# Attention and mixture-of-experts kernel: raw rows of v in the first chunk's coarse product, the local product with v stored with the neighbours innermost, and another order on ScalarE in the lead-in

## The chip, the cores and the metric

The kernel runs on one core of one Trainium2 chip. The metric is the device time of one execution in microseconds; less is better.

## The reference, cut to what matters

```python
# attention: q, k, v are (4, 8, 576, 64)
q_d = q.reshape(B, H, 144, 4, D).mean(axis=3)        # k_d, v_d likewise
out_d = softmax(scale * q_d @ k_d.T) @ v_d           # coarse attention
out_up = np.repeat(out_d, 4, axis=2)
mask = np.abs(pos[:, None] - pos[None, :]) < 4       # each row sees 7 neighbours
out_local = softmax(where(mask, scale * q @ k.T, -1e9)) @ v
x = (out_up + out_local) -> (2304, 512)
# experts: w_gate (512, 8), w1 (8, 512, 1024), w2 (8, 1024, 512)
P = exp(x @ w_gate - max); 8 rounds of row and column normalisation
out = sum over e of P[:, e:e+1] * (relu(x @ w1[e]) @ w2[e])
```

## The kernel before, in words

The 576 positions are taken in groups of four (144 groups for each batch and head). The rows of x are cut into six chunks of groups; the first two have 64 groups (256 rows of x), the next three 128. For a chunk the kernel makes the local attention (seven neighbours for each row, on VectorE, partly on GpSimd), the coarse attention (on TensorE with its softmax on VectorE and ScalarE), and the sum of both, x. The matrix products of the experts run on TensorE meanwhile, on the chunks whose x is ready.

**Experts.** A unit is one expert and 128 of its 1024 hidden columns. `mm1` multiplies x with a piece of w1 (12 matmuls into `psh`: x and w1 are each kept as a high part, `xh` and `w1h`, and a rest, `xl` and `w1l`), `mm2` with a piece of w2 (`psy`). The units of the first four experts run on the first chunk alone (32 units, 256 columns wide); the units after them on the first two chunks together (512 wide). The weights arrive as raw tiles `r`; ScalarE makes the high part (L193), GpSimd the rest (L200), or VectorE, where the planner finds that GpSimd would be late (L203). `hh` (ScalarE) and `hl` (VectorE) are the two parts of the hidden layer after the relu.

**The lead-in** is what comes before the first `psh` matmul: the whole attention of the first chunk. Its tiles in the order of the work: `psq` and `pssum` (sums over four rows of q and k, made by matmuls with the identity), copied by ScalarE to `qf` and `kz`; `pss`, the coarse scores; `nm`, their negated maxima (VectorE); `pp`, exponentials and then the normalised weights (ScalarE, with `sm` from VectorE between); `pst`, their transposes; `pt`, the copy of these (ScalarE); `psv`, the sums over four rows of v (L524), copied to `dv` (L529); `pso`, weights times `dv` (L595); `od`, its copy. Each comes twice, for the two halves hf of the heads. Beside this the local attention: products `prod` of q with neighbours of k (L274), their sums `sc` (L297), a softmax over seven neighbours, products of these weights with neighbours of v (L336), and their sums over the neighbours `lo` (L367). In the first chunk GpSimd makes three of the four products with v. `psx` (L771) transposes `lo`; `xs` adds `od` to it (L779); `xh` and `xl` are its two parts.

**What sets the order.** The program is written by a planner that runs on the host before: each piece of work is a Python generator (a thread) that yields the planned time at which it can go on, or `None` while it has to wait for another thread; at each turn the thread with the lowest time goes on. The planned times come from a clock for each engine (`dve`, `act`, `pool`, `pe`, with fixed costs). So each engine gets one list of instructions, which it executes in order. In the lead-in the threads are `w` (gate weights), `l` (local attention), `q`, `s0`, `s1` (sums of k), `v0`, `v1` (sums of v), `a`, `b` (coarse attention of the two halves) and `x`. After the lead-in the same threads go on between the units, at places that depend on the planned clocks; `pump` in `mm1` and `mm2` lets them in.

The lines that matter most:

```python
in_=pr[:, r0:r0 + nr].rearrange("p r w d -> p r d w"), axis=AX.X, op=ALU.add,   # L367 sum over w
d_sum[0, hf, 2] = (t_sb, done)                                                    # first_v, sums of v ready
vs, t_v = d_sum.pop((0, hf, 2))                                                   # first_d waits for them
while not x_ok(0):                                                                # the lead-in's loop
v_done = (0, 1, 2) in d_sum or 1 in v_set                                         # weights wait for the sums of v
```

## Time and profile before

| | |
|---|---|
| median of 3 runs | 1734.84 us (1732.46 to 1734.93) |
| the profiled execution's own time | 1733.57 us |
| its span in the profile | 1731.8 us |
| TensorE busy | 1691.7 us, 98% of the span |
| VectorE, GpSimd, ScalarE busy | 787.0, 676.9 and 494.8 us |
| first `psh` matmul, first `psy` matmul | at 48.96 us, at 58.26 us |

The profile gives each instruction's engine, line, tiles, start and length, and names what ended an idle time. Times are counted from the start of the span; the execution's own time is 1.8 us more than the span. [...]

### The profile page before, as it was taken

Reading aid. Unit: us, or ns where it says so; the run is one execution under the profiler, and the core shown is the slowest. Engines: PE = TensorE matmul, PEld = TensorE weight load, DVE = VectorE, ACT = ScalarE, POOL = GpSimd, SP = SyncE. Lnnn points to the kernel's source line nnn. Section 1 sums busy time; section 2 is a strip of 40 time slices with the busy share of each in tenths; the row PEclk is TensorE's granted clock in tenths of the full one; section 3 lists DMA queues with packets and bytes.
Section 4 is the critical chain, followed back from the end, with each engine's and each line's share of the span. In section 5 each row is a group of like instructions: output and inputs, shape, how many; then the busy total and the mean of one; then the engine's idle time right before and its main releaser. Section 6 shows DMA issues by size and latency. Waiting matters only on the chain.

```text
span 1731.8 us, 21860 instructions
## 1 busy us (share of the span) xinstructions
PE 1691.7 (98%) x8457; PEld 1405.0 (81%) x8457; DVE 787.0 (45%) x922; ACT 494.8 (29%) x1030; POOL 676.9 (39%) x479
## 2 busy tenths in 40 slices
PE   6988999999999999999999999999999999999998
PEld 4877888788788877888888888888888888888887
DVE  7678887798788784513433421121111111211112
ACT  1554443444344333331121131131131221311210
POOL 5889886587676554440040040040040220401300
PEclk7899999999999999999999999999999999999999
DMA  8786666677577533341251240030030120300101
GB/s 200 197 235 190 170 186 178 169 192 183 154 168 183 138 116 116 115 137 47 73 183 49 67 134 1 0 98 1 0 110 1 37 62 1 97 1 13 49 25 37
DMA packets 177609, 178.12 MB, mean 103 GB/s; under 512 B 10850, under 2 KB 127088, under 8 KB 177506
## 3 DMA queue, kind: packets, MB, share of 16 engines
q1 hardware_dynamic: 166754, 157.33, 34.2%
q10 hardware_dynamic: 10752, 19.40, 3.2%
q8 instruction: 66, 1.08, 0.3%
q14 instruction: 37, 0.30, 0.1%
HBM read 157.29 MB, written 19.40 MB: 102 GB/s over the span
## 4 chain that ended last, share of the span: by engine, by line
PE 78%; issue 10%; POOL 5%; DMA 5%; DVE 2%; ACT 0%; SPq 0%; POOLq 0%; ACTq 0%; DVEq 0%
PE psh L957 38%; PE psy L976 13%; PE psy L978 12%; PE psy L977 12%; DMA r<-in_moe_w_dram 3%; POOL w1l L200 2%; POOL w2l L200 2%; DVE lo L367 1%; POOL dr L449 1%; DMA dr<-in_k_dram 1%; DMA dr<-in_v_dram 1%; PE pss L673 0%; PE psg L808 0%; DMA lq<-in_q_dram 0%; PE psx L771 0%
## 5 line engine op out<-in xcount | busy, mean ns | idle before, releaser
L200 POOL TENSOR_TENSOR w1l<-r,w1h 128x512 fp32r<-128x512 f32 x192 | 280.3, 1460 | 867.6 <-ACT w1h L193 842.7
L966 DVE SCALAR_TENSOR_TENSOR hl<-psh,hh 128x512 fp32r<-128x512 f32 (+1 forms) x352 | 208.5, 592 | 851.7 <-ACT hh L963 851.6
L957 PE MATMUL psh<-xh,w1h 128*128 128x512 f32 (+1 forms) x1408 | 502.7, 357 | 2.7 <-ACT w1h L193 2.1
L957 PE MATMUL psh<-xl,w1h 128*128 128x512 f32 (+1 forms) x1408 | 497.6, 353 | 3.8 <-POOL xl L792 2.0
L957 PE MATMUL psh<-xh,w1l 128*128 128x512 f32 (+1 forms) x1408 | 497.4, 353 | 1.2 <-POOL w1l L200 1.2
L963 ACT ACTIVATE hh<-psh 128x512 fp32r<-128x512 f32 (+1 forms) x352 | 182.7, 519 | 981.2 <-PE psh L957 962.7
L976 PE MATMUL psy<-w2h,hh 128*128 128x512 f32 x1152 | 456.6, 396 | 0.1
L978 PE MATMUL psy<-w2h,hl 128*128 128x512 f32 x1152 | 451.8, 392 | 0.0
L977 PE MATMUL psy<-w2l,hh 128*128 128x512 f32 x1152 | 451.8, 392 | 0.0
L957 PEld LDWEIGHTS psh<-xh,w1h 128*128 128x128 f32 x1408 | 266.9, 190 | 47.0 <-ACT w1h L193 2.5
L957 PEld LDWEIGHTS psh<-xl,w1h 128*128 128x128 f32 x1408 | 267.2, 190 | 45.9 <-DVE xl L795 2.7
L957 PEld LDWEIGHTS psh<-xh,w1l 128*128 128x128 f32 x1408 | 267.1, 190 | 39.2 <-POOL w1l L200 1.8
L200 POOL TENSOR_TENSOR w2l<-r,w2h 128x512 fp32r<-128x512 f32 x183 | 272.5, 1489 | 42.5 <-ACT w2h L193 41.1
L978 PEld LDWEIGHTS psy<-w2h,hl 128*128 128x128 f32 x1152 | 216.4, 188 | 48.6 <-DVE hl L966 0.2
L976 PEld LDWEIGHTS psy<-w2h,hh 128*128 128x128 f32 x1152 | 216.9, 188 | 42.1 <-ACT hh L963 0.3
L977 PEld LDWEIGHTS psy<-w2l,hh 128*128 128x128 f32 x1152 | 216.8, 188 | 41.2
L193 ACT ACTIVATE w2h<-r 128x512 fp32r<-128x512 f32 x192 | 121.1, 630 | 166.1 <-POOL w1l L200 54.6
L367 DVE TENSOR_REDUCE lo<-prod 128x256 f32<-128x1792 f32 x36 | 123.8, 3441 | 0.3
L193 ACT ACTIVATE w1h<-r 128x512 fp32r<-128x512 f32 x192 | 120.1, 625 | 12.4 <-ACT sp L1144 6.0
L274 DVE TENSOR_TENSOR prod<-lq,lw 128x1792 f32<-128x1792 f32 x34 | 81.6, 2400 | 4.4 <-DMA lw<-in_k_dram 3.9
L336 DVE TENSOR_TENSOR prod<-lw,sc 128x1792 f32<-128x1792 f32 x33 | 79.4, 2405 | 0.6
L297 DVE TENSOR_REDUCE sc<-prod 128x28 f32<-128x1792 f32 x36 | 72.2, 2009 | 2.0 <-POOL prod L274 1.8
(121 smaller groups left out, 673.9 us busy)
## 6 DMA issues: line engine op xcount, KB each, us to landing
r<-in_moe_w_dram SPq DMA_DIRECT2D x384, 256.0 KB
spill<-sp ACTq DMA_DIRECT2D x56, 256.0 KB
s<-spill SPq DMA_DIRECT2D x56, 256.0 KB
dr<-in_k_dram SPq DMA_DIRECT2D x32, 144.0 KB
dr<-in_v_dram SPq DMA_DIRECT2D x32, 144.0 KB
dr<-in_q_dram SPq DMA_DIRECT2D x24, 144.0 KB
out_dram<-acc ACTq DMA_DIRECT2D x12, 256.0 KB
lw<-in_v_dram SPq DMA_DIRECT2D x4, 640.0 KB
```

The source lines that it names most:

```text
L193: nc.scalar.activation(out=h, in_=r, func=AF.Copy)
L200: nc.gpsimd.tensor_tensor(out=l, in0=r, in1=h.bitcast(F32), op=ALU.subtract)
L274: eng.tensor_tensor(out=pr[:, r0:r0 + nr], in0=with_free(qt[:, h, r0:], [(D, nr), (0, W), (1, D)]), in1=with_free(kt[:, h, r0:], [(D, nr), ...
L297: nc.vector.tensor_reduce(out=sc[:, h, r0:r0 + nr], in_=pr[:, r0:r0 + nr], axis=AX.X, op=ALU.add)
L336: eng.tensor_tensor(out=pr[:, r0:r0 + nr], in0=with_free(vt[:, h, r0:], [(D, nr), (D, W), (1, D)]), in1=with_free(sc[:, h, r0:], [(W, nr), ...
L367: nc.vector.tensor_reduce(out=ot[:, r0:r0 + nr, h % 2], in_=pr[:, r0:r0 + nr].rearrange("p r w d -> p r d w"), axis=AX.X, op=ALU.add,)
L957: nc.tensor.matmul(out=ps, lhsT=w[:, kk], rhs=x[:, kk], start=(i == 0), stop=(i == len(seq) - 1))
L963: nc.scalar.activation(out=hh, in_=ps, func=AF.Relu)
L966: nc.vector.scalar_tensor_tensor(out=hl, in0=ps, scalar=0.0, in1=hh.bitcast(F32), op0=ALU.max, op1=ALU.subtract)
L976: nc.tensor.matmul(out=y, lhsT=hh[:, ts], rhs=h2, start=(f == 0), stop=False)
L977: nc.tensor.matmul(out=y, lhsT=hh[:, ts], rhs=l2, start=False, stop=False)
L978: nc.tensor.matmul(out=y, lhsT=hl[:, ts], rhs=h2, start=False, stop=(f == NF - 1))
```

## The change

It has three parts. First, the coarse product of the first chunk (`pso`) no longer takes the sums of v over four rows but the raw rows: for each half and pair of heads it adds up eight matmuls for each of the two heads (two key halves times four rows) where there were two. The sums of v are still made, since the rest of the first batch uses them, but the threads `v0` and `v1` now wait until `od` of their half is made. Second, the local product with v is stored as (row, d, neighbour) instead of (row, neighbour, d): the product is written in steps of 28 bytes and the sum over the neighbours reads adjacent elements. Third, the order in the lead-in: the exponential of the local softmax waits (in the planner) until both `kz` are copied, the gate weights until both `od` are made, the conversion of expert weights may begin once `kz` is there instead of the sums of v, and the lead-in's loop ends only when all its threads are done.

```diff
             t = dve(112)
+            while u == 0 and len(k_set) < 2:
+                yield None
             nc.scalar.activation(out=sc3, in_=sc3, func=AF.Exp)
...
             def pv_prod(h, eng, pr, r0, nr, *deps):
                 eng.tensor_tensor(
-                    out=pr[:, r0:r0 + nr],
+                    out=with_free(pr[:, r0], [(W * D, nr), (1, W), (W, D)]),
...
                     nc.vector.tensor_reduce(
                         out=ot[:, r0:r0 + nr, h % 2],
-                        in_=pr[:, r0:r0 + nr].rearrange("p r w d -> p r d w"), axis=AX.X, op=ALU.add,
+                        in_=with_free(pr[:, r0], [(W * D, nr), (W, D), (1, W)]), axis=AX.X, op=ALU.add,
...
     def first_v(hf):
-        done = 0.0
+        while hf not in od_f:
+            yield None
         for p in range(2):
-            while (0, hf, p, 2) not in d_raw:
-                yield None
             raw, t_raw = d_raw.pop((0, hf, p, 2))
-            yield t_raw
+            yield max(t_raw, od_f[hf])
...
-            done = act(256, t)
-        d_sum[0, hf, 2] = (t_sb, done)
+            act(256, t)
+        v_set[hf] = t_sb
...
-        while (0, hf, 2) not in d_sum:
-            yield None
-        vs, t_v = d_sum.pop((0, hf, 2))
-        v_set[hf] = vs
-        yield max(t, t_v) + HOP
         ps = ps_a.tile([128, 2, Q0], F32, tag="a", name="pso")
         for p in range(2):
-            for i in range(2):
-                for kh in range(2):
+            while (0, hf, p, 2) not in d_raw:
+                yield None
+            raw, t_v = d_raw[0, hf, p, 2]
+            yield max(t, t_v) + HOP
+            rv = raw[0:HK].rearrange("p k h (a d) -> p k h a d", a=R)
+            for j in range(2 * R):
+                kh, r = divmod(j, R)
+                for i in range(2):
                     nc.tensor.matmul(
-                        out=ps[64 * i:64 * i + 64, p], lhsT=vs[0:HK, kh, 2 * p + i, :], rhs=pt[:, p, kh, i],
-                        start=(kh == 0), stop=(kh == 1),
+                        out=ps[64 * i:64 * i + 64, p], lhsT=rv[:, kh, i, r, :], rhs=pt[:, p, kh, i],
+                        start=(j == 0), stop=(j == 2 * R - 1),
                     )
-        t = pe(1.4, t, t_v)
+            t = pe(2.0, t, t_v)
...
         def first_w():
+            while len(od_f) < 2:
+                yield None
             yield t_wg + 1.0
...
-        while not x_ok(0):
+        lead = ("w", "q", "s0", "s1", "v0", "v1", "a", "b", "x")
+        while not all(th[nm].done for nm in lead):
...
-            v_done = (0, 1, 2) in d_sum or 1 in v_set
-            if n_cv[0] < 4 and v_done and max(w_raw[n_cv[0]][2], clk["act"], clk["pool"] - 1.0) <= r:
+            if n_cv[0] < 4 and len(k_set) == 2 and max(w_raw[n_cv[0]][2], clk["act"], clk["pool"] - 1.0) <= r:
```

**How it moves the instructions.** The rows below are each engine's list as the program has it (line, operation, tiles written and read, shape, count); lines of the changed kernel are two to five higher. On TensorE, from `psq` to the first `psh`, the list of the kernel before reads

```order
L475 MATMUL psq<-ident,lq 64x128 x16
L502 MATMUL pssum<-ident,dr 64x72 x64
L524 MATMUL psv<-dr,ident 72x256 x8
L543 MATMUL pss<-kz_99,qf 128x144 x2
L543 MATMUL pss<-kz_100,qf 128x144 x2
L524 MATMUL psv<-dr,ident 72x256 x8
L574 MATMUL pst<-ident,pp 72x128 x8
L595 MATMUL pso<-pt,dv 64x64 x16
L771 MATMUL psx<-ident,lo 128x64 x16
L957 MATMUL psh<-xh_85,w1h 128x256
```

and that of the change

```order
L477 MATMUL psq<-ident,lq 64x128 x16
L504 MATMUL pssum<-ident,dr 64x72 x64
L544 MATMUL pss<-kz_99,qf 128x144 x2
L544 MATMUL pss<-kz_100,qf 128x144 x2
L575 MATMUL pst<-ident,pp 72x128 x8
L597 MATMUL pso<-pt,dr 64x64 x64
L773 MATMUL psx<-ident,lo 128x64 x4
L525 MATMUL psv<-dr,ident 72x256 x8
L773 MATMUL psx<-ident,lo 128x64 x4
L525 MATMUL psv<-dr,ident 72x256 x8
L773 MATMUL psx<-ident,lo 128x64 x8
L959 MATMUL psh<-xh_85,w1h 128x256
```

The sixteen `psv` matmuls moved from ahead of `pst` to between the `psx` transposes, right ahead of the first `psh`, and `pso` has 64 matmuls instead of 16.

On VectorE, in the lead-in from the last step of the local softmax (`sc`, L326, and L328 in the change) to the sums `lo`, before:

```order
L326 TENSOR_TENSOR sc<-sc,mx 128x112
L336 TENSOR_TENSOR prod<-lw,sc 128x1792
L367 TENSOR_REDUCE lo<-prod 128x4x64 x2
L552 MEMSET sme 128x4
L553 TENSOR_REDUCE nm<-pss 128x2
L367 TENSOR_REDUCE lo<-prod 128x4x64
L552 MEMSET sme 128x4
L553 TENSOR_REDUCE nm<-pss 128x2
L562 TENSOR_REDUCE sm<-sme 128x2
L563 RECIPROCAL sm<-sm 128x2
```

and in the change:

```order
L328 TENSOR_TENSOR sc<-sc,mx 128x112
L553 MEMSET sme 128x4
L554 TENSOR_REDUCE nm<-pss 128x2
L553 MEMSET sme 128x4
L554 TENSOR_REDUCE nm<-pss 128x2
L338 TENSOR_TENSOR prod<-lw,sc 128x4x7x64
L563 TENSOR_REDUCE sm<-sme 128x2
L564 RECIPROCAL sm<-sm 128x2
L563 TENSOR_REDUCE sm<-sme 128x2
L564 RECIPROCAL sm<-sm 128x2
L369 TENSOR_REDUCE lo<-prod 128x4x64
```

Both `nm` moved ahead of VectorE's own product, and both `sm` from behind the third sum `lo` to ahead of the first.

On VectorE at the place where x of the second chunk is made (`xs` and `xl` with the width 256) and the units change from 256 to 512 columns (`hl`), before:

```order
L779 TENSOR_TENSOR xs<-psx,od 128x256
L966 SCALAR_TENSOR_TENSOR hl<-psh,hh 128x256
L779 TENSOR_TENSOR xs<-psx,od 128x256
L795 TENSOR_TENSOR xl_86<-xs,xh_85 128x256
L779 TENSOR_TENSOR xs<-psx,od 128x256
L274 TENSOR_TENSOR prod<-lq,lw 128x1792
L779 TENSOR_TENSOR xs<-psx,od 128x256
L297 TENSOR_REDUCE sc<-prod 128x28
L274 TENSOR_TENSOR prod<-lq,lw 128x1792
L966 SCALAR_TENSOR_TENSOR hl<-psh,hh 128x512
```

and in the change, where four more `hl` of 256 columns stand between these rows and the first of 512:

```order
L203 TENSOR_TENSOR w2l<-r_1563,w2h 128x512
L781 TENSOR_TENSOR xs<-psx,od 128x256
L968 SCALAR_TENSOR_TENSOR hl<-psh,hh 128x256
L781 TENSOR_TENSOR xs<-psx,od 128x256
L797 TENSOR_TENSOR xl_86<-xs,xh_85 128x256
L968 SCALAR_TENSOR_TENSOR hl<-psh,hh 128x256
L274 TENSOR_TENSOR prod<-lq,lw 128x1792
L968 SCALAR_TENSOR_TENSOR hl<-psh,hh 128x256
L297 TENSOR_REDUCE sc<-prod 128x28
```

The second chunk's x moved to six units ahead of its first use; in the list of TensorE the rest of the first batch's coarse attention (`psqk` to `pso` of the groups 64 to 143) moved with it, from units 16 to 30 to units 2 to 16.

## Rows read from the trace of the kernel before

**Rows 1.** The page's second part: busy tenths of TensorE and the granted clock of TensorE (PEclk), in 40 equal slices of the span.

```profile
PE   6988999999999999999999999999999999999998
...
PEclk7899999999999999999999999999999999999999
```

**Rows 2.** Busy time of each engine by stretch (first columns: the stretch, its length, then busy us and instruction count of PE, PEld, DVE, ACT and POOL, then the granted clock, the busy share of the DMA engines and GB/s).

```profile
60.00:70.00 10.00, 10.00 (x68) 9.07 (x67) 8.76 (x8) 5.13 (x10) 10.00 (x6) 1.00 0.70 172
...
100.00:150.00 50.00, 41.03 (x263) 35.45 (x261) 35.64 (x38) 27.64 (x70) 40.86 (x30) 0.97 0.76 219
150.00:200.00 50.00, 45.83 (x250) 36.55 (x251) 40.67 (x40) 20.94 (x52) 42.85 (x31) 0.97 0.69 181
200.00:300.00 100.00, 99.33 (x491) 81.25 (x490) 80.39 (x66) 42.50 (x95) 81.23 (x56) 1.00 0.69 182
```

**Rows 3.** The timeline of the lead-in, all engines (start us, length us, engine, line, operation, tiles, count; in brackets the idle time of the engine before it and what ended it). A row with a count merges equal neighbours.

```profile
16.88 5.74 PE L502 MATMUL pssum<-ident,dr 72*64 72x72 f32 x96 [1.34 <-DMA dr<-in_k_dram]
17.64 3.84 DVE L274 TENSOR_TENSOR prod<-lq,lw 128x1792 f32<-128x1792 f32 x1
...
26.62 0.45 ACT L508 ACTIVATE kz<-pssum 128x144 f32<-128x144 f32 x2
...
27.86 2.02 DVE L336 TENSOR_TENSOR prod<-lw,sc 128x1792 f32<-128x1792 f32 x1
...
28.96 7.07 PE L524 MATMUL psv<-dr,ident 72*72 72x256 f32 x16 [6.34 <-DMA dr<-in_v_dram]
...
35.82 2.07 PE L543 MATMUL pss<-kz,qf 128*128 128x144 f32 x8
...
37.73 3.62 PE L524 MATMUL psv<-dr,ident 72*72 72x256 f32 x16
...
41.79 1.32 ACT L567 ACTIVATE pp<-pp,sm 128x144 f32<-128x144 f32 x4
...
42.25 1.33 PE L574 MATMUL pst<-ident,pp 128*72 128x128 f32 x8 [0.90 <-ACT pp L567]
...
44.58 1.07 ACT L584 ACTIVATE pt<-pst 72x512 f32<-72x512 f32 x2
...
45.22 2.03 PE L595 MATMUL pso<-pt,dv 72*64 72x64 f32 x32 [1.64 <-ACT pt L584]
...
47.19 1.17 PE L771 MATMUL psx<-ident,lo 64*128 64x64 f32 x16
...
48.96 0.58 PE L957 MATMUL psh<-xh,w1h 128*128 128x256 f32 x1 [0.60 <-ACT xh L788]
...
58.26 0.40 PE L976 MATMUL psy<-w2h,hh 128*128 128x512 f32 x1
```

**Rows 4.** The instructions on the tile prod between 0 and 60 us (line, engine, operation, tiles, count, then min/median/max ns).

```profile
L297 DVE TENSOR_REDUCE sc<-prod x4: 2009/2020/2021, 11.9 to 23.5; 128x28 f32<-128x1792 f32 x4
L367 DVE TENSOR_REDUCE lo<-prod x4: 3246/3254/3294, 29.9 to 42.2; 128x256 f32<-128x1792 f32 x4
...
L336 POOL TENSOR_TENSOR prod<-lw,sc x3: 3182/3185/4977, 28.0 to 36.0; 128x1792 f32<-128x1792 f32 x3
...
L336 DVE TENSOR_TENSOR prod<-lw,sc x1: 2025/2025/2025, 27.9 to 27.9; 128x1792 f32<-128x1792 f32 x1
```

**Rows 5.** The granted clock in stretches of the lead-in (columns as in Rows 2).

```profile
16.00:23.00 7.00, 5.74 (x96) 5.53 (x96) 6.97 (x3) 0.29 (x1) 3.60 (x1) 0.59 0.88 197
...
36.00:38.00 2.00, 2.00 (x11) 1.93 (x10) 1.37 (x4) 0.86 (x4) 2.00 (x2) 0.57 1.05 201
...
45.00:47.30 2.30, 2.08 (x34) 1.96 (x36) 0.46 (x1) 1.86 (x6) 2.30 (x3) 0.50 1.08 223
```

**Rows 6.** Instructions of VectorE by line and shape between 550 and 1000 us, two reduces of the gate over the same 144 elements: L861 reads neighbouring elements, L867 reads in steps of 32 bytes.

```profile
L867 DVE TENSOR_REDUCE tmp<-lg 128x8 f32<-128x144 f32 x8 | 3.5, 432 | 0.3
...
L861 DVE TENSOR_REDUCE tmp<-lg 128x18 f32<-128x144 f32 x8 | 2.4, 302 | 0.2
```

**Rows 7.** Five-microsecond stretches of the first expert passes (columns as in Rows 2).

```profile
100.00:105.00 5.00, 3.32 (x21) 2.52 (x19) 4.56 (x4) 1.45 (x3) 4.92 (x4) 1.00 1.15 264
105.00:110.00 5.00, 2.88 (x17) 2.50 (x18) 3.23 (x3) 3.84 (x10) 4.05 (x4) 1.00 1.02 330
...
120.00:125.00 5.00, 2.67 (x11) 2.06 (x11) 3.70 (x9) 1.99 (x8) 2.26 (x3) 0.80 0.79 250
...
165.00:170.00 5.00, 2.87 (x16) 1.48 (x15) 3.88 (x3) 1.35 (x3) 3.85 (x4) 1.00 1.10 287
170.00:175.00 5.00, 3.75 (x14) 2.78 (x15) 4.96 (x4) 1.01 (x2) 4.64 (x5) 0.66 0.28 84
```

**Rows 8.** What TensorE waited for between 49 and 220 us (total us, times, longest us).

```profile
PE psh L957 <- POOL xl L792: 2.0, 2, 1.6
PE psh L957 <- DVE xl L795: 1.8, 1, 1.8
PE pst L702 <- ACT pp L682: 1.5, 1, 1.5
...
PE pst L702 <- ACT pt L707: 0.7, 1, 0.7
```

**Rows 9.** The timeline around 120 us, all engines (columns as in Rows 3).

```profile
118.28 1.34 DVE L203 TENSOR_TENSOR w2l<-r,w2h 128x512 fp32r<-128x512 f32 x1 [0.36 <-ACT w2h L193]
...
122.33 0.33 PE L702 MATMUL pst<-ident,pp 80*72 80x80 f32 x2 [3.33 <-DVE pp L693]
```

More of the change, by code (lines that the diff above doesn't have):

```diff
@@ L1101, in attention_moe_kernel @@
         ini_ctx.close()
-        for nm in ("w", "q", "s0", "s1", "v0", "v1", "a", "b", "x"):
-            assert th[nm].done
+        for nm in lead:
             del th[nm]
```

## The prediction

> **What bounds the kernel now.** I read the page by slices first: TensorE is busy in nine tenths or more from the third slice to the last but one, at a granted clock of 0.9 or more from the second on [rows 1]. By stretch it is then 99.3 of 100 us busy from 200 to 300 us, while VectorE has 80 us and GpSimd 81 [rows 2]. There a faster VectorE gives nothing. What an edit can move lies in two places. One is the lead-in: the first `psy` starts at 58.26 us [rows 3], and everything behind it shifts with that. The other is the stretch from 100 to 200 us, where TensorE is idle for 50 - 41.03 = 9.0 and 50 - 45.83 = 4.2 us [rows 2], 13.1 together; the five-microsecond rows show where [rows 7]. So the sum is: shift of the first `psy`, plus what the idle 13.1 us become.
>
> **The lead-in, step by step.** The exponential of the local softmax no longer stands ahead of the last two `kz` on ScalarE. They ran at 26.62, though `pssum` had ended at 16.88 + 5.74 = 22.62 [rows 3]; now they run at about 22.9, `pss` (2.07 us) ends near 25.3, and both `nm` follow the softmax on VectorE at 27.9, in 1.0 us. Then stands VectorE's own product, and here I see a new wait. GpSimd starts its first product at 28.0 [rows 4]. When a product of VectorE met one of GpSimd at 17.64 it took 3.84 us, not 2.02 [rows 3, 4]: it waited until GpSimd's ended. Before, VectorE came 0.1 us earlier and GpSimd's first product took 4.98 instead of 3.18 [rows 4]. Now GpSimd is first and VectorE waits until 28.0 + 3.2 = 31.2 and is done at 33.1. Behind it in its list are the two `sm` (some 0.6 us), and behind these wait `pp` (1.32), `pst` (1.33) and `pt` (1.07) [rows 3]; overlapped by halves as before (41.79 to 45.22, 3.4 us, less the conversions that stood among them), `pso` can start near 35.6, which is 9.6 us earlier than at 45.22.
>
> `pso` has 64 matmuls for 16. The 16 are 32 records in 2.03 us [rows 3], 63 ns each, at a clock of 0.50 [rows 5]; 128 records are 8.1 us, so it ends at 43.7 instead of 47.25. The reading of raw v in place of `dv` costs no wait, since v had landed for `psv` at 28.96 [rows 3].
>
> Now the `psv` matmuls, which ran while TensorE would have waited for VectorE and ScalarE, stand between the transposes, on TensorE's list ahead of the first `psh`. The first half took 7.07 us at the low clock, the second 3.62 at the high one [rows 3]. What clock they get is not in the trace, so both ends. The clock was at 0.50 in `pso` and through most of `psv`, and rose within the stretch 36 to 38 us while `psv` and `pss` ran; under `pssum`, in 16 to 23 us, it fell and did not rise again [rows 5]. I price the two halves as they ran before, the first low and the second high: `pso` until 43.7, one `psx` (1.17 / 4 = 0.3 us), 7.07, `psx`, 3.62, and two `psx`, which is 55.6. With both at the high clock the last `psx` ends at 51.8, with both at the low one at 59.0.
>
> From the end of the last `psx` (47.19 + 1.17 = 48.36) to the first `psy` (58.26) there were 9.9 us [rows 3]. [...] That leaves 5.3 us, and 60.9 for the first `psy`: **+2.6 us**, with the ends at 57.1 (-1.2) and, with the low clock all through, 59.0 + 8.7 = 67.7 (+9.4).
>
> **The reduces.** The sum over neighbours takes 3.25 us, that over d, which reads adjacent elements, 2.02 over as many [rows 4]. The changed one should take 2.0. In the lead-in VectorE then ends its `lo` near 41.8, ahead of TensorE, so this is hidden behind `pso`. After 200 us it is hidden behind a full TensorE. What it does between, with the moved order, is the second term.
>
> **The stretch from 100 to 200 us.** Three things go. The second chunk's x was made right ahead of its first use; TensorE was idle 2.1 + 1.3 us at 165 to 175 [rows 7], under the waits for `xl` [rows 8], and the clock at 0.66 over 5 us cost 1.7 more. With six units of 2.8 us ahead this goes: -5.1. At 122.33 `pst` waits 3.33 us for `pp` of VectorE, behind a run of L203 that the order now spreads [rows 9], and the clock of 0.80 over 5 us costs 1.0 [rows 7]: -4.3. What comes: the same coarse steps now stand in units 2 to 16, where GpSimd is full (10.00 of 10 us, [rows 2]). In their quieter place the second half's `pst` cost 1.5 + 0.7 us [rows 8]; I take this for each half, +4.4. The idle 1.7 + 2.1 us at 100 to 110 [rows 7] stay, since the loads of the third chunk stand at the same unit. **-5.0 us**; -9.4 if the new place costs nothing, -0.6 if it costs twice as much.
>
> **The strided write.** No row of this trace writes single elements in wide steps, so its price is bounded: nothing below (a gain has no source, the elements are as many), and above what reading in steps costs, 3.25 - 2.02 = 1.2 us, or by the two gate reduces (0.43 and 0.30 us over 144 elements, [rows 6]) 0.9 ns per element, 1.6 us. I take nothing, since both rows that pay are reads and the product's own reads stay as they are, and I keep the upper end as a rival with much weight.
>
> [...]
>
> **Sum.** +2.6 - 5.0 = -2.4 us on the execution of 1733.57 gives 1731.2. The median of three is 1.3 above that execution, and from there it is 1732.4. I predict **1732 us**, 0.16% under the median. Something within 0.2% (3.5 us) is about what a measurement of this kernel can't tell from no change.
>
> **The rivals.** *Forecast as above*, 42%, by itself 1726 to 1737 (a `psy` 3 us earlier or later, the new waits nothing to twice). *The write pays as the strided read does* (28%, slower). In the lead-in the first GpSimd product and VectorE's product are 1.2 to 1.6 us longer each and `pso` starts 2.8 us later. Between units 4 and 32 nine products of VectorE hold up GpSimd for 1.2 us more each; where it is full, about half of the time, TensorE follows: 5.5 us. 1731.2 + 8.3 = 1739.5. For it speak the strided reads [rows 4, 6]; against it, only that no row shows a write that pays. It decides if VectorE's product goes above 2.5 us uncontended. *The clock stays low until the experts' matmuls* (17%, slower by a little): the end at +9.4, 6.8 us more, 1738. For it speaks `pssum`, 5.7 us of work without a rise; against it, the rise while `psv` and `pss` ran [rows 5]. *The high clock for all of `psv` and no new waits* (13%, faster): -1.2 - 9.4, 1723. For it speaks that the 3.62 us ran so [rows 3]; against it, GpSimd's full stretch.
>
> **Range and chances.** The first case lies half on either side of -0.2%: 18% faster, 21% the same, 3% slower. The second gives 21% slower and 7% the same, the third 8% and 9%, the fourth 12% faster and 1% the same. Together 30% faster, 38% within 0.2%, 32% slower. 1724 to 1741 leaves out half of the fourth case and a third of the second with the end of the third, some 19%.
>
> **What would show it.** Right: `pso` starting at 35 to 37 us and lasting 8 us; VectorE's first product with v near 4 us long; `psv` between `psx` for 11 us; first `psy` at 60 to 63; L369 at 2.0 us; no wait for `xl` at the first 512-wide unit. Wrong: L338 on VectorE well over 2.5 us outside contention, a clock of 0.50 until 60 us, or TensorE idle by more than 12 us between 60 and 200.

## The result, and the profile after

The changed kernel takes 1752.58 us (median of 4 runs, 1749.25 to 1756.83) against 1734.88 us for the kernel before (median of 4). The ratio is 1.0106, with a 95% interval of 1.0081 to 1.0131: 17.7 us slower. The profiled execution took 1749.25 us, with a span of 1747.3 us, 15.5 us more than the span before.

The lead-in of the changed kernel, from its timeline (start us, length us, engine, line, operation, tiles, shape, records; in brackets the idle time before and what ended it):

```profile
21.97 2.29 PE L544 MATMUL pss<-kz,qf 128*128 128x144 f32 x8
...
26.31 0.45 DVE L554 TENSOR_REDUCE nm<-pss 128x2 f32<-128x288 f32 x1
...
27.27 3.38 DVE L338 TENSOR_TENSOR prod<-lw,sc 128x1792 f32<-128x1792 f32 x1
27.31 13.23 POOL L338 TENSOR_TENSOR prod<-lw,sc 128x1792 f32<-128x1792 f32 x3 [9.15 <-DMA dr<-in_v_dram]
...
31.44 1.92 PE L575 MATMUL pst<-ident,pp 128*72 128x128 f32 x8 [7.18 <-ACT pp L568]
...
33.29 7.10 PE L597 MATMUL pso<-pt,dr 72*64 72x64 f32 x128
...
40.93 7.10 PE L525 MATMUL psv<-dr,ident 72*72 72x256 f32 x16
...
48.58 7.10 PE L525 MATMUL psv<-dr,ident 72*72 72x256 f32 x16
...
55.61 0.70 PE L773 MATMUL psx<-ident,lo 64*128 64x64 f32 x8
...
63.70 0.40 PE L978 MATMUL psy<-w2h,hh 128*128 128x512 f32 x1
```

The coarse product `pso` begins at 33.29 us where it began at 45.22 [rows 3], but it takes 7.10 us for 2.03, and the sums of v behind it take 7.10 us for each half. The first `psy` comes at 63.70 us instead of 58.26 (5.4 us later). VectorE's product with v (L338, before L336) takes 3.38 us, for 2.02 before [rows 4], while GpSimd's first waits (6.53 us; its other two take 3.47 and 3.51).

By stretch, the kernel before (columns: length; busy us and records of PE, PEld, DVE, ACT, POOL; granted clock of TensorE as a share of the full one, DMA share, GB/s):

```profile
60.00:100.00 40.00, 39.84 (x254) 35.87 (x253) 30.63 (x32) 20.77 (x42) 39.93 (x25) 1.00 0.76 198
100.00:200.00 100.00, 86.86 (x513) 72.00 (x512) 76.31 (x78) 48.58 (x120) 83.71 (x60) 0.97 0.73 200
200.00:700.00 500.00, 498.44 (x2386) 404.69 (x2385) 388.64 (x337) 206.82 (x443) 339.47 (x231) 1.00 0.60 161
```

and the changed kernel:

```profile
63.70:100.00 36.30, 28.25 (x183) 24.07 (x181) 24.86 (x23) 16.03 (x41) 26.12 (x19) 0.95 0.52 140
...
100.00:200.00 100.00, 91.52 (x546) 78.22 (x546) 83.24 (x72) 49.04 (x108) 90.16 (x61) 0.98 0.75 208
200.00:700.00 500.00, 493.20 (x2363) 399.09 (x2363) 415.83 (x340) 208.28 (x452) 398.10 (x236) 1.00 0.62 162
```

TensorE's idle time is the length minus its busy time. From the first `psy` to 100 us it rises from 0.2 to 8.05 us (+7.9), from 100 to 200 us it falls from 13.14 to 8.48 (-4.7), from 200 to 700 us it rises from 1.56 to 6.80 (+5.2). By estimate, the length times the share of the clock that was not granted, the clock of 0.95 over 36.3 us costs 1.8 us more, and the one of 0.98 for 0.97 gives back 1.0. With the 5.4 us of the lead-in that is 14.6 of the 15.5 us. From 200 to 700 us GpSimd is busy for 398 us instead of 339 and VectorE for 416 instead of 389, though GpSimd's conversions are as many (226 for 227 from 64 to 700 us).

What TensorE waited for from 55 to 720 us (us in total, times, longest):

```profile
PE psy L980 <- DVE hl L968: 7.6, 5, 2.6
PE pst L704 <- DVE pp L695: 5.7, 7, 1.9
PE psqk L622 <- POOL dq L460: 3.4, 1, 3.4
PE psx L773 <- DVE lo L369: 3.3, 4, 1.2
```

The waits for `xl` before the first 512-wide unit [rows 8] are gone. TensorE now waits for `hl`, for which the kernel before had no wait worth a row, longer for `pp` (5.7 us for 4.2) and `lo` (3.3 for 0.7), all of VectorE, and longer, once, for `dq` of GpSimd (3.4 for 0.9).

### The profile page after: what moved, and what is told of

Read it like the earlier page. It is cut to its first block, busy times and chain, and to the rows that moved or that the text cites. A ratio compares the mean times of both kernels' runs of the same rounds, so it can differ in the third digit from the quotient of the medians.

```text
span 1747.3 us, 22045 instructions
## 1 busy us (share of the span) xinstructions
PE 1700.8 (97%) x8553; PEld 1410.6 (81%) x8553; DVE 813.0 (47%) x916; ACT 496.4 (28%) x1030; POOL 738.5 (42%) x485
## 3 DMA queue, kind: packets, MB, share of 16 engines
q1 hardware_dynamic: 166754, 157.33, 34.9%
## 4 chain that ended last, share of the span: by engine, by line
PE 74%; issue 8%; DVE 6%; DMA 5%; POOL 5%; SPq 1%; ACT 0%; POOLq 0%; ACTq 0%; DVEq 0%
PE psh L959 36%; PE psy L978 12%; PE psy L980 12%; PE psy L979 12%; DMA r<-in_moe_w_dram 3%; DVE prod L338 2%; POOL w1l L200 2%; POOL w2l L200 2%; DVE lo L369 1%; POOL prod L338 1%; DVE prod L274 1%; DMA dr<-in_q_dram 1%; DMA lw<-in_v_dram 1%; DVE hl L968 0%; DVE sm L691 0%
## 5 line engine op out<-in xcount | busy, mean ns | idle before, releaser
L200 POOL TENSOR_TENSOR w1l<-r,w1h 128x512 fp32r<-128x512 f32 x192 | 297.5, 1550 | 813.8 <-ACT w1h L193 806.1
L200 POOL TENSOR_TENSOR w2l<-r,w2h 128x512 fp32r<-128x512 f32 x186 | 302.4, 1626 | 34.8 <-ACT w2h L193 34.5
L980 PEld LDWEIGHTS psy<-w2h,hl 128*128 128x128 f32 x1152 | 216.7, 188 | 58.8 <-DVE hl L968 10.2
L338 DVE TENSOR_TENSOR prod<-lw,sc 128x1792 f32<-128x1792 f32 x33 | 143.1, 4336 | 0.6
L193 ACT ACTIVATE w1h<-r 128x512 fp32r<-128x512 f32 x192 | 120.2, 626 | 25.1 <-DMA r<-in_moe_w_dram 18.4
L274 DVE TENSOR_TENSOR prod<-lq,lw 128x1792 f32<-128x1792 f32 x34 | 95.3, 2802 | 2.9 <-DMA dr<-in_k_dram 2.4
L369 DVE TENSOR_REDUCE lo<-prod 128x256 f32<-128x1792 f32 x36 | 72.3, 2010 | 6.3 <-POOL prod L338 3.5
L451 POOL TENSOR_TENSOR dr<-dr 72x512 f32<-72x512 f32 (+1 forms) x38 | 67.2, 1768 | 18.3 <-DMA dr<-in_q_dram 15.7
```

Of the source, the lines that this page charges most:

```text
L193: nc.scalar.activation(out=h, in_=r, func=AF.Copy)
L200: nc.gpsimd.tensor_tensor(out=l, in0=r, in1=h.bitcast(F32), op=ALU.subtract)
L274: eng.tensor_tensor(out=pr[:, r0:r0 + nr], in0=with_free(qt[:, h, r0:], [(D, nr), (0, W), (1, D)]), in1=with_free(kt[:, h, r0:], [(D, nr), ...
L338: eng.tensor_tensor(out=with_free(pr[:, r0], [(W * D, nr), (1, W), (W, D)]), in0=with_free(vt[:, h, r0:], [(D, nr), (D, W), (1, D)]), in1= ...
L369: nc.vector.tensor_reduce(out=ot[:, r0:r0 + nr, h % 2], in_=with_free(pr[:, r0], [(W * D, nr), (W, D), (1, W)]), axis=AX.X, op=ALU.add,)
L451: add(out=rv[:, :, 0, :], in0=rv[:, :, 0, :], in1=rv[:, :, 1, :], op=ALU.add)
```

## The experiments

All thirteen, with the ratio to the kernel before of the same chip, and from each profile the first `psy` and TensorE's idle time by stretch. These last four columns come from one execution of each kernel, which is not always near its median: it took 1750.2 us in e1, 1756.7 in e2, 1738.9 in e6 and 1742.3 in e9. The first `psy` also scatters: before, e2, e7, e8, e11, e12 and e13 have the same list of matmuls in the lead-in, and theirs lies anywhere from 56.1 to 59.1 us.

| run | median us | ratio, 95% interval | first `psy` | idle 60-100 | 100-200 | 200-700 |
|---|---|---|---|---|---|---|
| before | 1734.9 | 1 | 58.3 | 0.2 | 13.1 | 1.6 |
| after | 1752.6 | 1.0106 (1.0081 to 1.0131) | 63.7 | 8.1 | 8.5 | 6.8 |
| e1_old_layout | 1742.5 | 1.0056 (1.0036 to 1.0076) | 64.3 | 5.8 | 10.4 | 4.4 |
| e2_layout_only | 1752.2 | 1.0101 (1.0086 to 1.0115) | 59.1 | 0.1 | 16.0 | 10.8 |
| e3_order_only | 1735.6 | 1.0006 (0.9998 to 1.0015) | 58.6 | 0.1 | 11.1 | 2.5 |
| e4_sums_early | 1743.3 | 1.0063 (1.0047 to 1.0079) | 62.8 | 5.8 | 11.1 | 2.2 |
| e5_raw_late_order | 1738.7 | 1.0024 (1.0012 to 1.0036) | 60.8 | 0.1 | 13.3 | 1.6 |
| e6_sums_early_order | 1742.4 | 1.0042 (1.0027 to 1.0057) | 60.6 | 7.1 | 7.6 | 3.1 |
| e7_layout_first | 1733.8 | 1.0002 (0.9992 to 1.0012) | 56.1 | 0.1 | 11.4 | 1.5 |
| e8_near_reduce | 1734.9 | 1.0003 (0.9994 to 1.0012) | 58.8 | 0.1 | 13.4 | 1.2 |
| e9_q_early | 1737.4 | 1.0013 (0.9997 to 1.0030) | 63.2 | 2.7 | 12.8 | 3.2 |
| e10_mid_order | 1754.8 | 1.0114 (1.0101 to 1.0127) | 60.1 | 4.1 | 18.4 | 7.4 |
| e11_two_input | 1750.9 | 1.0090 (1.0077 to 1.0103) | 58.3 | 0.9 | 14.8 | 10.0 |
| e12_short_product | 1732.1 | 0.9995 (0.9986 to 1.0004) | 56.9 | 0.0 | 12.4 | 0.7 |
| e13_more_reduce | 1735.9 | 1.0007 (0.9998 to 1.0016) | 58.6 | 0.6 | 13.5 | 1.0 |

### Which part costs: e1, e2, e3, e4

**e1_old_layout**, the changed kernel without its second part:

```diff
-  out=with_free(pr[:, r0], [(W * D, nr), (1, W), (W, D)]),
+  out=pr[:, r0:r0 + nr],
...
-  in_=with_free(pr[:, r0], [(W * D, nr), (W, D), (1, W)]), axis=AX.X, op=ALU.add,
+  in_=pr[:, r0:r0 + nr].rearrange("p r w d -> p r d w"), axis=AX.X, op=ALU.add,
```

> The changed kernel with the local product with v stored again as (row, neighbour, d): contiguous write, sum over the neighbours in steps; instruction order as in the changed kernel. Theory W (the strided write is most of the loss: VectorE's product is 3.38 us for 2.02, and hl and pp stand behind it): 8 to 12 us under the changed kernel, 1741 to 1745 us; no wait of psy for hl above 1 us in all; L338 on VectorE back to 2.0 us uncontended, L369 at 3.25. Theory O (the order and the sums of v on the path are most of it): at most 3 us under, 1750 us, with the first psy at 62 to 63 us and the waits at 65 to 100 us as before.

It took 1742.5 us, 10 us under the changed kernel: as theory W had it in size, but its waits of `psy` for `hl` stayed (10.0 us in 3), against W. So a second cause was left, and e4 to e9 look for it.

**e2_layout_only**, the kernel before with the reverse of that diff and nothing else.

> The kernel before with only the layout of the local product with v changed: strided write, adjacent read; instruction order as in the kernel before. Theory W: the first psy 1.5 to 3 us later than 58.26, TensorE idle 4 us more from 200 to 700 us, waits of psy for hl of 3 us or more, in all 8 to 12 us slower, 1743 to 1747 us. Theory O: 0 to 3 us slower, 1735 to 1738 us.

1752.2 us: the layout alone costs 17.5 us, more than W had said and as much as the whole change. The order of instructions is that of the kernel before. Nearly nothing of it is in the lead-in (+0.8 us). The idle time grows by 2.9 us from 100 to 200 us and by 9.2 us from 200 to 700 us, and the granted clock is 0.88 instead of 0.97 from 100 to 200 us, which by estimate is worth 6 us (over TensorE's busy time) to 9 us (over the whole stretch). A part of that is scatter between executions: e3, e8 and e13, as fast as the kernel before, show 0.91 there.

**e3_order_only**, the kernel before with the third part alone (both `while` loops, the condition of the conversion, the loop's end). **e4_sums_early** is e1 with the sums of v made when v lands:

```diff
-        while hf not in od_f:
-            yield None
         for p in range(2):
-            raw, t_raw = d_raw.pop((0, hf, p, 2))
-            yield max(t_raw, od_f[hf])
+            while (0, hf, p, 2) not in d_raw:
+                yield None
+            raw, t_raw = d_raw[0, hf, p, 2]
+            yield t_raw
```

> The kernel before with only the changed order of the lead-in (exponential behind both kz, gate weights behind both od, conversion of weights from kz on, loop until all threads are done); the coarse product still takes the sums of v and the layout is the old one. Theory W: the order by itself costs nothing: first psy within 2 us of 58.26, total within 3 us of the kernel before (1732 to 1738 us). Theory O, if the order is what hurts: the idle time of TensorE from 60 to 100 us, none in the kernel before, is 5 us or more here too, and the total 1740 us or more.

> The changed kernel with the old layout, and the sums of v made when v lands, as in the kernel before, instead of behind od; the coarse product still takes raw rows, 64 matmuls for 16. If the sums standing between the transposes are what makes the lead-in longer (theory O), the first psy comes 4 us earlier than in the changed kernel (near 59 to 60 us) and the total falls 4 us against the one with the old layout alone. Theory W: the same first psy as with the old layout alone, within 1.5 us, since the sums take the same time at another place.

e3 is the kernel before to within what can be measured: the third part costs nothing by itself. e4 took as long as e1 (1743.3 and 1742.5 us). Where the sums of v stand moved the first `psy` by 1.5 us (62.8 for 64.3), less than it scatters, and the total not at all. So the 8 us between e3 and e4 belong to the raw rows, or to what they do to the rest of the program.

### The raw rows: the matmuls or the order they bring, e5 and e6

The planner gives `pso` of raw rows a cost of 4.0 us for each half, where it had 1.4. That moves TensorE's planned clock, and with it a rule of `pump`: GpSimd's thread, which makes the sums of q for the second chunk, goes on only when GpSimd's planned clock is less than 1 us ahead of TensorE's. With the higher cost the second chunk's coarse steps stand in units 3 to 17, with the lower one in units 17 to 31. So the cost alone switches the order, whatever the matmuls are:

```diff
# e5_raw_late_order, on e4
-            t = pe(2.0, t, t_v)
+            t = pe(0.7, t, t_v)
# e6_sums_early_order, on e3
-        t = pe(1.4, t, t_v)
+        t = pe(4.0, t, t_v)
```

> The kernel with raw rows, old layout and sums of v made when v lands (1743.3 us), with one number changed: the planner's cost of the coarse product, 0.7 for 2.0 us. The second chunk's coarse steps then stand in units 17 to 31 again, as in the kernel before, not in units 3 to 17; the matmuls are the same. Theory P (the 48 matmuls more for each half are what costs): as without the change, 1741 to 1745 us. Theory Q (the earlier place of the second chunk's steps costs): the idle time of TensorE from 60 to 100 us falls from 5.8 to under 1 us and the total to 1737 to 1740 us, what is left over the kernel with the order alone (1735.6 us) being the longer lead-in.

> The kernel with only the order of the lead-in changed (1735.6 us; coarse product from the sums of v, old layout), with one number changed: the planner's cost of the coarse product, 4.0 for 1.4 us, what the raw rows were given. The second chunk's coarse steps then stand in units 3 to 17. Theory P: 1734 to 1738 us, since no matmul is added. Theory Q: TensorE idle 4 to 6 us between 60 and 100 us, waits of psy for hl near 10 us, and 1739 to 1743 us. My own forecast, that this place gives 5 us, says 1730 us.

The totals fall where theory Q had them in both (in e6 the idle time is above its 4 to 6 us, and the waits of `psy` for `hl` are 7.6 us for its 10). With the raw rows and the old order (e5) the idle time from 60 to 100 us is 0.1 us and the total 1738.7; with the sums and the early order (e6) it is 7.1 us and the total 1742.4. The longer coarse product costs some 3 us (e5 to e3; their intervals touch, and the first `psy` is 2.2 us later), the earlier place 5 to 7 us (e4 to e5, e6 to e3). I had forecast that the place gives 5 us.

What happens there shows in the changed kernel (GpSimd's and VectorE's rows, with TensorE's at `psqk` and at the late `psy`):

```profile
69.77 1.26 POOL L451 TENSOR_TENSOR dr<-dr 80x512 f32<-80x512 f32 x1 [10.67 <-DMA dr<-in_q_dram]
71.10 0.72 POOL L460 TENSOR_TENSOR dq<-dr 80x256 f32<-80x256 f32 x1
71.78 1.29 POOL L200 TENSOR_TENSOR w1l<-r,w1h 128x512 fp32r<-128x512 f32 x1
71.88 0.36 PE L622 MATMUL psqk<-ident,dq 80*128 80x80 f32 x2 [3.40 <-POOL dq L460]
...
75.17 7.26 DVE L274 TENSOR_TENSOR prod<-lq,lw 128x1792 f32<-128x1792 f32 x1
...
79.25 1.29 POOL L200 TENSOR_TENSOR w1l<-r,w1h 128x512 fp32r<-128x512 f32 x1
...
82.35 0.41 DVE L968 SCALAR_TENSOR_TENSOR hl<-psh,hh 128x256 fp32r<-128x256 f32 x1
82.81 0.50 PE L980 MATMUL psy<-w2h,hl 128*128 128x512 f32 x1 [0.97 <-DVE hl L968]
```

The sum of q now stands at the head of GpSimd's list right behind the lead-in, but its load is issued only at the end of the lead-in. GpSimd waits for it for 10.67 us. Meanwhile the conversions behind it become ready, and GpSimd then runs them without a gap, 1.28 us each. VectorE's product L274, 2.02 us by itself, starts in the middle of this run and takes 7.26 us: it ends at 82.43, 1.9 us, about its own length, behind the run's end at 80.54; `hl` stands behind it, and `psy` behind `hl`.

### Is it the late load? e9 and e10

**e9_q_early** is e6 with the load of q issued ahead of the second chunk's local loads; only SP's list changes. **e10_mid_order** is e3 with the rule's bound at 2 us instead of 1.

```diff
# e9_q_early, on e6
         d_limit[0] = len(d_loads)
+        d_load()
# e10_mid_order, on e3
-            if can("p", now) and clk["pool"] < now + 1:
+            if can("p", now) and clk["pool"] < now + 2:
```

> The kernel of e6 (sums of v in the coarse product, old layout, second chunk's coarse steps in units 3 to 17; +7 us), with the loads of q for the second chunk issued ahead of the second chunk's local loads instead of at the end of the lead-in; the lists of all engines but SP are the same. In e6 GpSimd waited 8.26 us for this load with the sum of q at the head of its list, then ran seven conversions without a gap, and VectorE's product beside them took 9.16 us for 2.02, with hl behind it. Theory L (the late load starts this): no wait of GpSimd for q above 2 us, no product of VectorE above 5 us before 100 us, TensorE idle under 2 us from 60 to 100 us (7.1 in e6), and 5 to 8 us less than e6: 1734 to 1737 us. Theory C (GpSimd is simply too full there for the sums of q): the waits of psy for hl stay near 7 us and the total near 1742 us.

> The kernel with only the changed order of the lead-in (old layout, sums of v in the coarse product, 1735.6 us), with GpSimd's thread let in when its planned clock is under 2 us ahead of TensorE's, not 1 us: the second chunk's coarse steps then stand in units 6 to 21, behind five more conversions on GpSimd than in e6. Theory L: the load of q has landed by then; no 8 us wait, and what I forecast for the earlier place comes out, TensorE idle 3 to 6 us less between 100 and 200 us than in the kernel before: 1730 to 1734 us. Theory C: 1737 us or more.

The same place in e6 (GpSimd's sum of q, VectorE's product, `hl`, `psy`):

```profile
64.41 1.28 POOL L451 TENSOR_TENSOR dr<-dr 80x512 f32<-80x512 f32 x1 [8.26 <-DMA dr<-in_q_dram]
...
69.17 9.16 DVE L274 TENSOR_TENSOR prod<-lq,lw 128x1792 f32<-128x1792 f32 x1
...
78.26 0.41 DVE L968 SCALAR_TENSOR_TENSOR hl<-psh,hh 128x256 fp32r<-128x256 f32 x1
...
78.72 0.52 PE L980 MATMUL psy<-w2h,hl 128*128 128x512 f32 x1 [3.75 <-DVE hl L968]
```

and in e9:

```profile
53.36 0.63 ACT L193 ACTIVATE w1h<-r 128x512 fp32r<-128x512 f32 x1 [4.49 <-DMA r<-in_moe_w_dram]
...
55.54 0.26 ACT L605 ACTIVATE od<-pso 128x128 f32<-128x128 f32 x1
...
58.82 1.47 POOL L451 TENSOR_TENSOR dr<-dr 80x512 f32<-80x512 f32 x1
...
70.42 2.56 DVE L274 TENSOR_TENSOR prod<-lq,lw 128x1792 f32<-128x1792 f32 x1
```

In e9 the sum of q waits for nothing, the product takes 2.56 us, and the idle time from 60 to 100 us falls from 7.1 to 2.7 us (theory L had under 2). So at this place it is the late load that starts the waits. For the total it is less clear. The median falls from 1742.4 to 1737.4 us, at the edge of theory L's 1734 to 1737, but both kernels spread widely, 1731 to 1748 and 1730 to 1743 us, their intervals touch, and of the two profiled executions that of e9 is the slower. It shows two losses that L had not said. The first `psy` is at 63.2 us, 2.6 us later than in e6: ScalarE waits 4.49 us for a weight tile (0.94 in e6), and the second `od` behind it comes at 55.54 us (52.23 in e6). And from 100 to 200 us TensorE is idle for 12.8 us instead of 7.6, with a wait of `psy` for `hl` of 5.0 us at 129 us, behind a conversion on VectorE (L203) of 5.97 us that takes 1.78 us in e6. How much of the place's 5 to 7 us is the late load stays open.

e10 refutes the hope that went with it. It took 1754.8 us, the slowest of all, though the raw rows and the layout are out of it. GpSimd waits for q for 1.3 us at most, but from 100 to 200 us TensorE is idle for 18.4 us at a clock of 0.90, with waits for `pp` (4.6 us at 125 us) and `hl` (5.3 us at 178). One of its rows shows the same wait on an instruction of 16 elements a lane (0.17 us by itself) which reads only one tensor (GpSimd's rows beside it):

```profile
111.82 1.29 POOL L200 TENSOR_TENSOR w2l<-r,w2h 128x512 fp32r<-128x512 f32 x1
...
112.47 3.18 DVE L326 TENSOR_SCALAR mx<-mx 128x16 f32<-128x16 f32 x1
...
113.07 1.29 POOL L200 TENSOR_TENSOR w1l<-r,w1h 128x512 fp32r<-128x512 f32 x1
...
114.33 1.29 POOL L200 TENSOR_TENSOR w2l<-r,w2h 128x512 fp32r<-128x512 f32 x1
115.58 0.74 POOL L460 TENSOR_TENSOR dq<-dr 72x256 f32<-72x256 f32 x1
```

It ends at 115.65, with the last of GpSimd's conversions (115.62), though GpSimd's next instruction, a sum, follows without a gap. Which of its waits makes e10 20 us slower was not tried; it shows that the earlier place is not good as such.

### How the layout costs: e7, e8, e11, e12, e13

**e7_layout_first** has the new layout in the first chunk only (`if u == 0`), **e8_near_reduce** the new sum without the new product (its sums take elements that do not belong together, so it serves for its time alone, as do e11, e12 and e13):

```diff
# e8_near_reduce, on the kernel before
-  in_=pr[:, r0:r0 + nr].rearrange("p r w d -> p r d w"), axis=AX.X, op=ALU.add,
+  in_=with_free(pr[:, r0], [(W * D, nr), (W, D), (1, W)]), axis=AX.X, op=ALU.add,
```

> The kernel before with the new layout of the local product with v in the first chunk only (there GpSimd makes three of its four products). If the lead-in pays, as my rival put it, the first psy comes 2.8 us later and the total is 1737 to 1738 us. If nearly all of the 17.5 us of the layout lies in VectorE's products behind the lead-in, the total is within 2 us of the kernel before (1734 to 1737 us).

> The kernel before with the product with v written as before (adjacent) and the sum over seven reading seven adjacent elements, so that it adds up the wrong elements in the same number: the saving of the layout without its price. Each of 36 sums takes 2.0 for 3.25 us on VectorE. If VectorE's time is hidden behind TensorE, as I forecast, 0 to 2 us faster (1733 to 1735 us). If the sums stand ahead of hl and pp on VectorE and so on TensorE's path, 4 to 8 us faster (1727 to 1731 us).

Both measure as the kernel before. The lead-in pays nothing for the layout. The sums on VectorE take 2.0 us for 3.25 in the first chunk and for 3.46 in the mean of the 32 behind it, and this gains nothing: that time is hidden. So, by what is left, all 17.5 us come from VectorE's longer product behind the lead-in. VectorE's own time hardly changes there: at their shortest product and sum take 3.38 + 1.99 us in the changed kernel, which has the layout of e2, and 2.01 + 3.38 in the kernel before. The layout turns time of a sum into time of a product. Rows of e2 at one such product:

```profile
203.54 1.29 POOL L200 TENSOR_TENSOR w2l<-r,w2h 128x512 fp32r<-128x512 f32 x1
203.70 4.63 DVE L336 TENSOR_TENSOR prod<-lw,sc 128x1792 f32<-128x1792 f32 x1
204.79 3.99 POOL L458 TENSOR_TENSOR dk<-dr 72x256 f32<-72x256 f32 x1
...
213.35 0.75 POOL L458 TENSOR_TENSOR dk<-dr 72x256 f32<-72x256 f32 x1
```

The product waits until GpSimd's conversion ends at 204.8 and then takes 3.5 us; GpSimd's next sum, 0.75 us by itself, waits until the product ends at 208.3. In these rows one runs at a time. By estimate, 3.4 - 2.0, the longer product then takes 1.4 us from GpSimd as well. The sum over seven is not held: with adjacent reads it takes 1.99 to 2.05 us in all 36 instances of the changed kernel, beside GpSimd's products (31.05 us, 2.00) or not, and 2.01 us in the mean of 32 in e2, e8, e11 and e13.

**e11_two_input** and **e13_more_reduce** put 1.3 us behind each of VectorE's products, on e8: once a second product over 42 columns, once a sum. **e12_short_product** cuts the product to 32 of 64 columns.

```diff
# e11_two_input, on e8, in pv_prod behind the product
+                if eng is nc.vector:
+                    eng.tensor_tensor(
+                        out=with_free(pr[:, r0], [(W * D, nr), (D, W), (1, 42)]), ...
# e13_more_reduce, on e8, behind pv_prod
+                        nc.vector.tensor_reduce(
+                            out=ot[:, r0:r0 + nr, h % 2, 0:42],
+                            in_=with_free(pr[:, r0], [(W * D, nr), (W, 42), (1, W)]), axis=AX.X, op=ALU.add,
+                        )
# e12_short_product, on the kernel before, VectorE's products behind the first chunk
+                        out=with_free(pr[:, r0], [(W * 32, nr), (32, W), (1, 32)]), ...
```

> The kernel before with the sum over seven reading adjacent (wrong) elements, 2.0 for 3.25 us, and behind each of VectorE's products with v a second product over 42 of 64 columns, 1.3 us, which writes the same values again: all writes are adjacent, and VectorE's work is as long as with the new layout alone (1752.2 us, +17.5). Theory T (what costs is the longer time in which VectorE's two-input product and GpSimd shut each other out, however it arises): 1744 to 1753 us. Theory S (it is the wide steps of the write, beyond its duration): 1735 to 1739 us.

> As e11 (sum over seven reading adjacent, wrong elements, 2.0 for 3.25 us), but the 1.3 us put behind each of VectorE's products with v are a sum over seven (one input, overwritten by the next one), not a second product: the same time, at the same place in VectorE's list. e11 was 16 us slower than the kernel before. If that came from hl, pp and lo standing 1.3 us further back in VectorE's list, whatever fills the time, this is 13 to 17 us slower as well, 1748 to 1752 us. If it came from VectorE's products and GpSimd's work shutting each other out, this costs 0 to 4 us, 1734 to 1738 us, and the mean of VectorE's product, 2.4 us, stays.

> The kernel before with VectorE's product with v cut behind the first chunk to 32 of 64 columns, about 1.0 us less for each of 32 products; the sum over seven takes 256 columns as before, from what is there, so the values of x are wrong. It asks whether the price of the two-input time goes both ways. The longer product (1.3 us more) cost 16 to 17.5 us. If the price is even, this gives 8 to 13 us: 1722 to 1727 us. If before most of the two-input time was already hidden behind TensorE, so that only time added costs, 0 to 3 us: 1732 to 1735 us.

VectorE's groups from 64 to 700 us in e11 (line, tiles, shapes, count; busy us, mean ns; idle before):

```profile
L336 DVE TENSOR_TENSOR prod<-lw,sc 128x1792 f32<-128x1792 f32 x32 | 81.2, 2538 | 0.5
L343 DVE TENSOR_TENSOR prod<-lw,sc 128x1176 f32<-128x1176 f32 x32 | 72.4, 2263 | 1.1
```

and in e13:

```profile
L336 DVE TENSOR_TENSOR prod<-lw,sc 128x1792 f32<-128x1792 f32 x32 | 79.2, 2476 | 0.5
...
L366 DVE TENSOR_REDUCE lo<-prod 128x168 f32<-128x1176 f32 x32 | 44.1, 1378 | 3.1 <-PE psx L775 2.0
```

e11 writes nothing in steps and costs 16 us, as the layout does; e13 has the same 1.3 us at the same place in VectorE's list and costs 1.2 us (interval from -0.3 to 2.8). So it is neither the steps as such nor the place of `hl` and `pp` behind a longer list. It is the time in which a product of VectorE and GpSimd's work shut each other out: the second product over 1176 elements took 1.38 us at its shortest, but 2.26 in the mean (e11), the sum over as many 1.38 in the mean (e13). Behind 200 us nearly all of TensorE's waits in e11 and e2 are for `lo`, `hl` and `pp` of VectorE. Whether VectorE's waiting or the delay of GpSimd is the larger part of the price was not separated. e12 shows that this is a price in one direction: 1.0 us less for each product (mean 1.33 us) measures as nothing (-0.9 us, interval -2.4 to 0.7).

## Why the prediction was wrong

The time, 1752.6 us, is above the range (1724 to 1741) by 12 us. All three signs named for a wrong prediction came: L338 on VectorE at 3.38 us uncontended, a clock of 0.50 until 60 us, and TensorE idle for 16.5 us from 60 to 200 us. By the steps:

- **Step by step through the lead-in.** Right that `kz`, `pss` and `nm` come earlier and that `pso` starts some 12 us earlier (33.3; I had 35.6). That it starts 2.3 us ahead of my time is luck: I had VectorE's own product wait for GpSimd's first, but GpSimd waited for the load of v until 27.31 and VectorE began 0.04 us ahead. In e1, with the same lists, GpSimd began first, VectorE's product took 4.70 us, and `pso` started at 34.9. `pso` took 7.1 us for my 8.1. The sums of v ran at the low clock in both halves, 14.2 us for my 10.7, so the last `psx` ended at 56.3, near my 55.6, with two errors against each other. My split, the first half low and the second high, was read from one execution: with the same list of matmuls the second half took 3.6 us in the kernel before and in e7, but 7.0 us in e2, e8, e11 and e13. The clock was 0.50 until 62.5 us, which was the third rival's condition, so the matmuls up to the first `psy` took 7.4 us for my 5.3. My 5.3 had 3.4 us less for the higher clock, half of 0.213 us for each of 32 matmuls, and no run shows that half: in both kernels matmuls of 256 columns start 0.213 us apart at a clock of 0.50 and 0.12 us apart at 1.00, which for 32 makes 3.0 us. It also had 1.25 us less of waiting in the first twelve `psh`, which took 5.1 us before and 4.15 here. The first `psy` came at 63.7 instead of 60.9: the term of +2.6 measured +5.4.
- **The reduces**: 2.0 us each and hidden; e8 shows it.
- **The stretch from 100 to 200 us**: -5.0 forecast, -4.7 in that stretch, and the waits for `xl` and the 3.3 us for `pp` are gone as said. That the numbers agree is partly luck: the 3.8 us of idle time at 100 to 110 us that I had let stay are gone too, and 5.7 us of waits for `hl` and `lo` came that I had not. And the same move put +7.9 us of idle time into 60 to 100 us, where I had looked for none. I had priced the new place by the waits of `pst`; I did not see that GpSimd would stand before a load that is issued only at the end of the lead-in, nor that the conversions then run in one piece. By e6 the place costs 7 us by itself, instead of giving 5.
- **The strided write** is the step that failed most. I took it as nothing because no row showed a write that pays. It pays 1.36 us on VectorE (3.38 for 2.02, e7 and after), within my bounds of 1.2 to 1.6, and 0.3 us on GpSimd, whose three products of the first chunk cost nothing (e7). Over the kernel that is 17.5 us by itself (e2) and 10 us on the changed order (e1 to after), where I had 0.
- **The second rival** had the mechanism, but its price was 8.3 us (and its 1739.5 us lacks the 1.3 us by which the forecast goes from the profiled execution to the median, as the other rivals' times do). Its 2.8 us in the lead-in were 0 (e7). Its 5.5 us counted only nine products in units 4 to 32; behind 200 us I took VectorE's time as hidden behind a full TensorE. That holds for its time alone (e8, e13), but not for time in which it and GpSimd shut each other out (e11): TensorE's idle time grows by 9.2 us there in e2, by 5.2 in the changed kernel.
- **The parts do not add.** The layout costs 17.5 us on the kernel before and 10 on the order that the raw rows bring (e1 to after); the other parts cost 8 alone. Why is open. A reason that was not tried: in e2 the clock fell to 0.88 between 100 and 200 us, where the second chunk's x is late; with the early order it stayed at 0.98.

## What to carry to other kernels

An engine's busy share did not tell here what longer work on it costs: 1.3 us more behind each of VectorE's products cost 16 us over the kernel as a product, which GpSimd's work held up (2.26 us in the mean for 1.38, e11), and 1.2 us as a sum, which it did not (1.38 us, e13). Ask which of the two an instruction is, and price the time on both engines. A price may have one direction: 1.3 us more of a product cost 16 us, 1.0 us less gave nothing (e12). And a planner's cost that is changed with the work it stands for can move other work across a threshold; undo the cost alone to tell the two apart.

## What the runs showed of the hardware

Where VectorE's products met GpSimd's work, one waited, but how long it was held differs. Mostly it came in after one instruction of the other (25 of the 30 products that were held by 0.14 us or more behind the lead-in, in the trace of the kernel before). One such place there:

```profile
64.83 1.30 POOL L200 TENSOR_TENSOR w2l<-r,w2h 128x512 fp32r<-128x512 f32 x1
...
65.26 2.76 DVE L274 TENSOR_TENSOR prod<-lq,lw 128x1792 f32<-128x1792 f32 x1
66.08 3.09 POOL L200 TENSOR_TENSOR w1l<-r,w1h 128x512 fp32r<-128x512 f32 x1
```

The product waits until the conversion ends at 66.1 and then takes its 2.0 us; the next conversion, which follows without a gap, is held in its turn (3.09 us for 1.28). In e6 the product that starts at 69.17 is held over six conversions in a run, each of 1.26 to 1.29 us as if alone, and ends 9.16 us later (the last of them ended at 76.45). In e10 the one-input instruction L326 is held over three (3.18 us for 0.17). What decides between the two is open. The sums over seven were not held (L369 in the changed kernel, 1.99 to 2.05 us), nor those over d (L297, 2.00 to 2.02 us in both kernels).

Writing fp32 elements in steps of 28 bytes cost VectorE 0.76 ns per element more ((3.38 - 2.02) / 1792), and GpSimd 0.16 to 0.18 ns (3.47 and 3.51 us in the changed kernel for 3.18).
